# The second feed-forward of an attention and two feed-forward kernel moved into the list scheduler as single operations

## The chip, the cores and the metric

One core of a Trainium2 chip runs the whole program. The metric is the device time of one execution in microseconds; of several executions the median is given. Engine names follow the profile: PE is TensorE, DVE is VectorE, ACT is ScalarE, POOL is GpSimd, SP is SyncE, which issues nearly all DMAs here.

## The reference

Linear attention without a softmax, an RMS norm, a feed-forward with the maximum of three products, and a second feed-forward with a squared ReLU:

```python
kv = np.einsum('bhsd,bhse->bhde', k, v)            # batch 8, heads 8, seq 576, head_dim 64
out = np.einsum('bhsd,bhde->bhse', q, kv)
rms = np.sqrt(np.mean(out * out, axis=-1, keepdims=True) + 1e-06)
x = out / rms * g_norm                             # then 4608 tokens x 512
h = np.maximum(np.maximum(x @ w1, x @ w2), x @ w3) # 512 x 768
x = h @ w_out                                      # 768 x 512
h = x @ w_in                                       # second feed-forward, 512 x 2048
g = s * np.maximum(h, 0.0) ** 2 + b
return g @ w_out                                   # 2048 x 512
```

## The kernel before

All products are made in three matmuls of rounded parts: each operand is split into a high part (ScalarE copies it into the shorter format, `hi_part`, or the first half of `split`, L160) and a low part (the difference, `lo_part`, or the second half of `split`, L161), and a product is high x high + high x low + low x high.

**The first part** (attention and first feed-forward) works on nine blocks of 512 token columns, 22 positions each. Every operation is a *job* (L70): a position, an engine, a price in us, a function, and the names it reads, writes and allocates. `arrange` (L73) is a list scheduler: it derives the dependencies, keeps a clock for each engine, and takes at every step, on the engine that can begin first, the ready job with the lowest position. An allocation in a ring of n slots (`SIZE`) depends on the users of the one n before it. A job's end is its begin plus its price plus a lag (2.0 us for DMAs, 0.1 us otherwise, unless given). The order so found is issued with the order of PE, SP, DVE, ACT and POOL all kept as written (L138). Jobs with a position below `CUT` go there; this ends in the ninth block.

**The second feed-forward** uses a Strassen scheme with seven products instead of eight. *The w_in stage*: 20 groups `G`, four weight groups g for each of five pairs of token blocks (four pairs 512 columns wide, the last block's pair 256). `left` makes weight operands from a 1 MB load of `wd[g]` (`q_load`), `x_sums` and `right` make token operands from `x1_load`, `product` (L880) does one of seven products in 12 matmuls, `combine` (L897) empties its accumulators: products 0 to 2 are copied to `cs` by ScalarE, products 3 to 5 are added to these copies by VectorE, then ReLU and square, and `keep` stores the result in `gd`. There are two sets of four PSUM banks; within a group products 0, 2, 4 and 6 use the bank pair "a" one after another, so product 6 waits for the adds of product 4. `bias_load`, `bias_add`, `bias_sums` and `bias_out` add up rows of w_out in the middle of this stage. *The w_out stage*: ten halves `H` (eight 512 wide, two 256 wide), seven products of 24 matmuls. `z_load` brings the kept results back, `z_right` (L950) makes one operand in one of six slots `HS` (for products 2 and 3 with a sum on VectorE before), and every sixth low part is done by GpSimd (L960). `z_product` (L962) multiplies; `z_combine` (L975) adds up. In odd halves GpSimd also adds the earlier half's result to the copies of products 0 to 2 (L991). `put` (L1032) transposes a finished pair on VectorE and stores it in four DMAs; for the last, half-wide pair it turns it by matmuls on PE.

All of this was entered by `at(position, function)` in the hand-written list `plan`. `run` (L135) sorts it by position together with the jobs left over from the first part, and issues it with only the order of PE and SP kept (L142); the order of DVE, ACT and POOL is found by the language's own scheduler at compile time.

Of the kernel before, what the change touches and what calls it, by code (L numbers as in the profile page):

```python
# [30 lines left out]
def attention_max_ffn_relu2_ffn(ctx: ExitStack, tc, q, k, v, g_norm, w1, w2, w3, wo, wi, w2o, s, b, out):  # L31
# [14 lines left out]
    B, H, S, D = q.shape  # L46
    DM = H * D
# [16 lines left out]
    plan, jobs = [], []  # L64
    SIZE = {"g": 4, "t": 2, "st": 2, "qt": 2, "o": 2, "kvc": 3, "k": NP, "v": NP, "cgc": 2}

    def at(pos, fn, *args):
        plan.append((pos, len(plan), fn, args))
# [4 lines left out]
    def arrange(todo):  # L73
# [5 lines left out]
        for n, (_, _, _, _, _, _, r, w, a, _) in enumerate(todo):  # L79
# [18 lines left out]
            deps = {d for d in deps if d[0] != n}  # L98
# [4 lines left out]
        for n, e in enumerate(todo):  # L103
            if not need[n]:
                for eng in e[2].split("/"):
                    heaps.setdefault(eng, []).append(n)
# [25 lines left out]
        assert len(out) == len(todo)  # L132
        return [todo[n] for _, n in out]

    def run():  # L135
        order = sorted(jobs, key=lambda e: e[:2])
        n = sum(e[0] < CUT for e in order)
        with tc.manual_schedule(engines={EngineType.PE, EngineType.SP, EngineType.DVE, EngineType.Activation, EngineType.Pool}):  # L138
            for e in arrange(order[:n]):
                e[4](*e[5])  # L140
        todo = sorted(plan + [(e[0], e[1] - len(jobs), e[4], e[5]) for e in order[n:]], key=lambda e: e[:2])
        with tc.manual_schedule(engines={EngineType.PE, EngineType.SP}):  # L142
            for _, _, fn, args in todo:
                fn(*args)
# [415 lines left out]
    def plan_conv(kk, src, pos, load, a, pr, slot=None, store=None):  # L560
# [11 lines left out]
        if store is None:  # L572
            job(pos, "ACT", 0.63, conv_hi, key, slot, r=[tr + ":t"], w=[f"W_{kk}:0"], a=[(slot, f"W_{kk}")])
            job(pos, "DVE", 0.69, conv_lo, key, r=[tr + ":t", f"W_{kk}:0"], w=[f"W_{kk}:1"])
        else:
            job(store, "SP", 1.1, conv_store, key, r=[tr + ":t"])
# [114 lines left out]
    def plan_g2_out(j, n, pos):  # L691
        job(pos, "ACT", 0.6, g2_out, j, n, r=[f"g2.{j}.{n}"], w=[f"x1.{j}.{n}"], a=[("st", f"x1.{j}.{n}")])
        job(pos + 0.2, "SP", 1.1, x1_store, j, n, r=[f"x1.{j}.{n}"])
# [84 lines left out]
    XS = ["l0", "l1", "l6", "l7", "l2", "l3", "l4", "l5"] + HS  # L778

# [9 lines left out]
    def bank(parity, nm):  # L789
        return (psg, p2["psum"])[parity % 2].tile([P, N], F32, tag="g", name=nm)  # L790

    def tmp(nm):
        return p2["pool"].tile([P, N], F32, tag="c", bufs=6, name=nm)

    turn = [0]

    def stage2(nm):
        turn[0] += 1
        return base.tile([P, N], F32, tag=("t", "st")[turn[0] % 2], bufs=2, name=nm)
# [4 lines left out]
    add, sub = ALU.add, ALU.subtract  # L804
# [3 lines left out]


    def q_load(g, into):  # L810
        raw = into()
        st["wq", g] = raw
        if len(raw) == 1:
            nc.sync.dma_start(out=raw[0], in_=wd[g])
        else:
            for i, r in enumerate(raw):
                nc.sync.dma_start(out=r, in_=wd[g][:, 2 * i:2 * i + 2])

    def quarter(g, n):
        raw = st["wq", g]  # L820
        return raw[0][:, n] if len(raw) == 1 else raw[n // 2][:, n % 2]

    def left(g, i):
        a11, a12, a21, a22 = (quarter(g, n) for n in range(4))
        s_ = st.setdefault(("S", g), {})

        def make(n, x, op, y):
            s_[n] = tmp(f"s{n}_{g}")
            tt(nc.vector, s_[n], x, op, y)

        if i == 1:
            make(3, a11, sub, a21)
        elif i == 2:
            make(1, a21, add, a22)
            make(2, s_[1], sub, a11)
            make(4, a12, sub, s_[2])
        f = {0: a11, 3: a22, 5: a12}.get(i)
        f = s_[{1: 3, 2: 2, 4: 1, 6: 4}[i]] if f is None else f
        w = wt["q", g, i] = slot(WS[g % 4][i], f"w_q_{g}_{i}")
        split(w[:, 0], w[:, 1], f, nc.vector)  # L840
# [3 lines left out]
    def width(q):  # L844
        return N if q < NQ - 1 else N // 2

    def x1_load(q):
        n = width(q)
        raw = [base.tile([P, KD, N], F32, tag=tg, name=f"{tg}1_{q}") for tg in ("xh", "xl")]
        for i, r in enumerate(raw):  # L850
            src = x1d[2 * q + i] if q < NQ - 1 else x1d[2 * q][:, :, i * n:(i + 1) * n]
            nc.sync.dma_start(out=r[:, :, :n], in_=src)
        p2["raw", q] = raw

    def x_sums(q, k):
        n = width(q)
        b11, b12, b21, b22 = (p2["raw", q][c][:, r * HK + k, :n] for r in range(2) for c in range(2))
        t3, t2, t4 = (tmp(f"t{m}_{q}_{k}")[:, :n] for m in (3, 2, 4))
        tt(nc.vector, t3, b22, sub, b12)
        tt(nc.vector, t2, t3, add, b11)  # L860
        tt(nc.vector, t4, b21, sub, t2)
        tt(nc.vector, b12, b12, sub, b11)
        p2["t", q, k] = (b11, t3, t2, t4, b12, b21, b22)

    def right(q, i, k):

        n = width(q)
        if n == N:
            x = slot(XS[2 * i + k], f"x_q_{q}_{i}_{k}")
        else:  # L870
            if k == 0:
                p2["x2", i] = slot(XS[2 * i], f"x_q_{q}_{i}")
            x = p2["x2", i][:, :, k * n:(k + 1) * n]
        p2["x", q, i, k] = x
        f = p2["t", q, k][i]
        split(x[:, 0], x[:, 1], f, nc.vector)

    BANK = "abababca"[:5] + "ca"

    def product(G, q, g, i):  # L880
# [3 lines left out]
        for m in range(2):  # L884
            if new:
                st["ps", BANK[i], m] = bank(G + (i == 5), f"ps_{BANK[i]}_{G}_{m}")
        w = wt["q", g, i]
        for k in range(HK):
            x = p2["x", q, i, k]
            for m in range(2):  # L890
                ps = st["ps", BANK[i], m][:, :n]
# [5 lines left out]
    def combine(G, q, g, i):  # L897


        n = width(q)  # L900
        for m in range(2):
            ps = st["ps", BANK[i], m][:, :n]
            if i < 3:
                s_ = st["cs", i, m] = p2["pool"].tile([P, N], F32, tag="s", bufs=9, name=f"cs_{G}_{i}_{m}")[:, :n]
                act(out=s_, in_=ps, func=AF.Copy)  # L905
                continue
            if i < 6:
                h = st["cs", 5 - i, m]
                tt(nc.vector, h, ps, add, h)
            else:  # L910
                h = stage2(f"r_{G}_{m}")[:, :n]
            if i < 6 and m == 0:
                stt(out=h, in0=h, scalar=0.0, in1=h, op0=ALU.max, op1=ALU.mult)
            else:
                act(out=h, in_=ps if i == 6 else h, func=AF.Relu)
                act(out=h, in_=h, func=AF.Square)
            st["r", i, m] = h
            if i == 6:
                d = st["r", 7, m] = stage2(f"d_{G}_{m}")[:, :n]
                tt(nc.vector, d, st["r", 4, m], sub, h)  # L920
                tt(nc.vector, h, h, sub, st["r", 5, m])

    def keep(q, g, i):
        for m in range(2):
            nc.sync.dma_start(out=gd[q][:, {5: 0, 4: 1, 3: 2, 7: 3, 6: 4}[i], 2 * g + m, :width(q)], in_=st["r", i, m])
# [6 lines left out]
    def z_load(H, i, u):  # L932
# [4 lines left out]
        t = tmp(f"z_{H}_{u}") if i == 1 else slot(GS[i][u], f"z_{H}_{i}_{u}", F32)  # L937
# [12 lines left out]
    def z_right(H, i, k_):  # L950
        n, z = width(H // 2), lambda i_: p2["z", H, i_, k_]
        if i in (2, 3):
            if i == 2:
                tt(nc.vector, z(1), z(1), add, z(0))
            else:
                tt(nc.vector, z(1), z(5), sub, z(1))
        f = z(1 if 0 < i < 4 else i)
        o = 28 * H + 4 * i + k_
        x = hs["z", i, k_] = slot(HS[o % M1], f"zx_{o}")
        split(x[:, 0, :n], x[:, 1, :n], f, nc.gpsimd if o % 6 == 5 else nc.vector)  # L960

    def z_product(H, i, k_):  # L962
        n, new = width(H // 2), i in (0, 1, 5)
        kk = 4 * (H % 2) + k_
        w, x = wt["q", 4 + kk // 2, i], hs["z", i, k_]
        for m in range(2):
            if new and k_ == 0:
                st["ps", BANK[i], m] = bank(H + (i == 5), f"zs_{BANK[i]}_{H}_{m}")
            ps = st["ps", BANK[i], m][:, :n]
            c = slice((2 * (kk % 2) + m) * P, (2 * (kk % 2) + m + 1) * P)  # L970
            for e, (a, b_) in enumerate(((0, 0), (0, 1), (1, 0))):
                nc.tensor.matmul(ps, lhsT=w[:, a, c], rhs=x[:, b_, :n], start=new and k_ == 0 and e == 0,  # L972
                                 stop=k_ == 3 and e == 2, skip_group_check=True)

    def z_combine(H, i):  # L975
        n, more = width(H // 2), H % 2

        def acc(i_, m):
            c = int(i_ in (4, 6))
            if ("o", H // 2, c) not in p2:  # L980
                tg = ("xh", "xl")[c]
                p2["o", H // 2, c] = base.tile([P, KD, N], F32, tag=tg, name=f"{tg}o_{H}")
            return p2["o", H // 2, c][:, 2 * (i_ in (3, 4)) + m, :n]

        for m in range(2):
            ps = st["ps", BANK[i], m][:, :n]
            if i < 3:
                s_ = st["cs", i, m] = p2["pool"].tile([P, N], F32, tag="s", bufs=9, name=f"zc_{H}_{i}_{m}")[:, :n]
                act(out=s_, in_=ps, func=AF.Copy)  # L989
                if more:  # L990
                    tt(nc.gpsimd, s_, s_, add, acc(5 - i, m))  # L991
            elif i < 6:
                tt(nc.vector, acc(i, m), ps, add, st["cs", 5 - i, m])
            elif more:
                tt(nc.vector, acc(i, m), ps, add, acc(i, m))
            else:
                act(out=acc(i, m), in_=ps, func=AF.Copy)
            if i > 2 and more:
                act(out=acc(i, m), in_=acc(i, m), func=AF.Identity, scale=sb_s,  # L999
# [148 lines left out]
```

## Time and profile before

| | |
|---|---|
| median of three executions | 1399.04 us (1398.34 to 1402.06) |
| the profiled execution | 1398.18 us, span in the profile 1396.3 us |
| PE busy | 1370.8 us, 98% of the span |
| DVE busy | 890.1 us, 64% |
| ACT busy | 745.9 us, 53% |
| POOL busy | 235.7 us, 17% |
| granted PE clock | full in all of the span but its last slices |
| DMA | 202.51 MB, 145 GB/s on average |

The page gives each engine's busy time, the share in slices of the span, and groups of instructions with their mean duration and the idle time before them. A matmul's record overlaps with the next one's: the start-to-start distance is its pace, the record is longer. A line number can be that of a helper: L802 is every `tt` (add or subtract), L160 and L161 are the two halves of `split`.

### The profile page before, as it was taken

How to read it: one execution, taken by the hardware profiler on the slowest of the kernel's cores; microseconds unless marked ns; L12 is line 12 of the kernel's file. 1: busy time of each engine (PE TensorE's matmuls, PEld its weight loads, DVE VectorE, ACT ScalarE, POOL GpSimd, SP SyncE). 2: the span in 40 equal slices, each digit the busy share in tenths (PEclk: the TensorE clock that was granted, in tenths of full speed). 3: DMA queues.
4: the chain of work that ended last, by engine and by line, in shares of the span. 5: the costliest groups of instructions: out<-in, count | busy, mean ns of one | idle time of the engine just before them, and what ended most of it. 6: DMA issues, size and time to landing. Idle time of an engine off the chain costs nothing. (4 is left out here: it accounts for less than half of the span.)

```text
span 1396.3 us, 19558 instructions
## 1 busy us (share of the span) xinstructions
PE 1370.8 (98%) x7056; PEld 1121.7 (80%) x7056; DVE 890.1 (64%) x1413; ACT 745.9 (53%) x1320; POOL 235.7 (17%) x175
## 2 busy tenths in 40 slices
PE   7999999999999999999999899999999999999997
PEld 4777888888888888888888789887888888888887
DVE  5984636263635462454756757568877978888884
ACT  6864424342524353333646466556675656566565
POOL 0001213131212222211000000000012314141412
PEclk9999999999999999999999999999999999999999
DMA  9987281818364321030355635544684454544441
GB/s 281 269 178 146 83 171 46 190 55 174 71 163 83 98 68 38 1 121 17 142 196 188 226 135 199 181 151 163 214 296 152 143 194 152 193 140 145 158 143 38
DMA packets 221328, 202.51 MB, mean 145 GB/s; under 512 B 117168, under 2 KB 175536, under 8 KB 219056
## 3 DMA queue, kind: packets, MB, share of 16 engines
q1 hardware_dynamic: 221072, 201.02, 48.7%
q8 instruction: 55, 0.90, 0.3%
q14 instruction: 41, 0.34, 0.1%
q10 hardware_dynamic: 160, 0.26, 0.0%
HBM read 126.79 MB, written 74.45 MB: 144 GB/s over the span
## 5 line engine op out<-in xcount | busy, mean ns | idle before, releaser
L164 PE MATMUL g<-xh,w_w 128*128 128x512 f32 x648 | 255.2, 394 | 0.0
L166 PE MATMUL g<-xh,w_w 128*128 128x512 f32 x648 | 252.9, 390 | 0.7 <-DVE w_w L285 0.7
L165 PE MATMUL g<-xl,w_w 128*128 128x512 f32 x648 | 252.6, 390 | 0.0
L160 ACT ACTIVATE zx<-z 128x512 fp32r<-128x512 f32 (+1 forms) x280 | 161.2, 587 | 123.1 <-PE zs_a L972 34.2
L894 PE MATMUL ps_a<-x_q,w_q 128*128 128x512 f32 (+1 forms) x960 | 209.9, 370 | 4.2 <-DVE cs L802 4.1
L972 PE MATMUL zs_a<-zx,w_q 128*128 128x512 f32 (+1 forms) x960 | 203.9, 369 | 0.5 <-POOL zx L161 0.3
L894 PEld LDWEIGHTS ps_a<-x_q,w_q 128*128 128x128 f32 x960 | 167.4, 188 | 37.9 <-DVE cs L802 6.7
L161 DVE TENSOR_TENSOR zx<-z,zx 128x512 fp32r<-128x512 f32 (+1 forms) x234 | 172.2, 753 | 34.7 <-ACT zx L160 34.3
L972 PEld LDWEIGHTS zs_a<-zx,w_q 128*128 128x128 f32 x960 | 167.8, 188 | 32.1 <-POOL zx L161 0.7
L534 DVE TENSOR_TENSOR h<-g,h 128x512 f32<-128x512 f32 x108 | 74.6, 691 | 143.0 <-PE g L166 139.0
L161 POOL TENSOR_TENSOR zx<-z,zx 128x512 fp32r<-128x512 f32 (+1 forms) x46 | 64.2, 1397 | 592.4 <-DMA gd<-cs 380.9
L164 PEld LDWEIGHTS g<-xh,w_w 128*128 128x128 f32 x648 | 121.6, 188 | 27.4 <-issue 0.8
L166 PEld LDWEIGHTS g<-xh,w_w 128*128 128x128 f32 x648 | 121.6, 188 | 27.0 <-DVE w_w L285 1.2
L165 PEld LDWEIGHTS g<-xl,w_w 128*128 128x128 f32 x648 | 121.7, 188 | 25.2 <-DVE xl L285 0.2
L285 POOL TENSOR_TENSOR h<-h,h 128x512 fp32r<-128x512 f32 x40 | 55.1, 1378 | 454.8 <-ACT h L282 454.8
L894 PE MATMUL ps_b<-x_q,w_q 128*128 128x512 f32 (+1 forms) x480 | 106.4, 369 | 1.8 <-ACT cs L905 1.2
L282 ACT ACTIVATE h<-h 128x512 fp32r<-128x512 f32 x54 | 34.0, 630 | 134.5 <-DVE h L534 133.7
L972 PE MATMUL zs_b<-zx,w_q 128*128 128x512 f32 (+1 forms) x480 | 103.9, 371 | 2.0 <-DVE zx L161 2.0
L972 PEld LDWEIGHTS zs_b<-zx,w_q 128*128 128x128 f32 x480 | 83.9, 188 | 19.0 <-DVE zx L161 3.2
L894 PEld LDWEIGHTS ps_b<-x_q,w_q 128*128 128x128 f32 x480 | 83.9, 188 | 18.3 <-ACT cs L905 1.9
L164 PE MATMUL g<-h,w_o 128*128 128x512 f32 x216 | 84.6, 392 | 0.0
L165 PE MATMUL g<-h,w_o 128*128 128x512 f32 x216 | 84.1, 389 | 0.0
(176 smaller groups left out, 1980.3 us busy)
## 6 DMA issues: line engine op xcount, KB each, us to landing
z<-gd SPq DMA_DIRECT2D x64, 512.0 KB
gd<-cs SPq DMA_DIRECT2D x96, 256.0 KB
z<-gd SPq DMA_DIRECT2D x48, 256.0 KB
x1d<-x SPq DMA_DIRECT2D x36, 256.0 KB
raw_w<-in_moe_w_dram SPq DMA_DIRECT2D x18, 511.0 KB
k<-in_k_dram SPq DMA_DIRECT2D x32, 256.0 KB
v<-in_v_dram SPq DMA_DIRECT2D x32, 256.0 KB
wd<-tr_p SPq DMA_DIRECT2D x32, 256.0 KB
```

The source lines that it names most:

```text
L160: act(out=hi, in_=src, func=AF.Copy)
L161: eng.tensor_tensor(out=lo, in0=src, in1=hi.bitcast(F32), op=ALU.subtract)
L164: nc.tensor.matmul(ps, lhsT=w[:, 0, sl], rhs=xh, start=first, stop=False)
L165: nc.tensor.matmul(ps, lhsT=w[:, 0, sl], rhs=xl, start=False, stop=False)
L166: nc.tensor.matmul(ps, lhsT=w[:, 1, sl], rhs=xh, start=False, stop=last)
L282: act(out=out, in_=src, func=AF.Copy)
L285: eng.tensor_tensor(out=out, in0=src, in1=hi.bitcast(F32), op=ALU.subtract)
L534: nc.vector.tensor_tensor(out=st["h", m], in0=ps, in1=st["h", m], op=ALU.max)
L894: nc.tensor.matmul(ps, lhsT=w[:, a, c], rhs=x[:, b_], start=new and k == 0 and e == 0, stop=k == HK - 1 and e == 2, skip_group_check=True)
L972: nc.tensor.matmul(ps, lhsT=w[:, a, c], rhs=x[:, b_, :n], start=new and k_ == 0 and e == 0, stop=k_ == 3 and e == 2, skip_group_check=True)
```

## The change

`plan`, `at` and the second half of `run` go away. Every operation of the second feed-forward becomes a job of its own, with price, names read, written and allocated; the functions are cut into single operations for that (`split` into `left_hi` and `left_lo`, `combine` into `comb_copy`, `comb_add`, `comb_sq`, `comb_d` and `comb_e`, and so on). `arrange` gets a second argument: the jobs before it are done and only give names. Engine orders of all five engines are now kept in the second part too. Positions stay as they were, but for `z_right`, which goes from 2.4 to 3 ahead of its product. In `z_lo` and in the sums of `z_comb` VectorE takes GpSimd's place. In the half-wide halves two operands share one of the six slots `HS`.

```diff
-    def arrange(todo):
+    def arrange(todo, done=0):
...
-            deps = {d for d in deps if d[0] != n}
+            deps = {d for d in deps if done <= d[0] != n} if n >= done else ()
...
-            if not need[n]:
+            if n >= done and not need[n]:
...
-        todo = sorted(plan + [(e[0], e[1] - len(jobs), e[4], e[5]) for e in order[n:]], key=lambda e: e[:2])
-        with tc.manual_schedule(engines={EngineType.PE, EngineType.SP}):
-            for _, _, fn, args in todo:
-                fn(*args)
+            open_late()
+            for e in arrange(order, n):
+                e[4](*e[5])
...
+    def cost(eng, n):
+        return {"ACT": 0.62, "DVE": 0.69, "POOL": 1.35}[eng] if n == N else {"ACT": 0.43, "DVE": 0.42, "POOL": 0.75}[eng]
...
+    def plan_q_load(pos, g, *tags):
+        two = len(tags) > 1
+        job(pos, SQ_, 3.4, q_load, g, tags, r=[f"wd{g}:{n}" for n in range(4)], w=[qk(g, n) for n in range(4)],
+            a=[(tag, f"wq{g}{'ab'[i]}") for i, tag in enumerate(tags)], lag=3.0)
...
+        job(pos, A, 0.62, left_hi, g, i, r=[f], w=[w + ":0"], a=[(WS[g % 4][i], w)])
+        job(pos, V, 0.69, left_lo, g, i, r=[f, w + ":0"], w=[w + ":1"])
...
+            job(pos, SQ_, 3.4 if q < NQ - 1 else 1.7, x1_load, q, i, r=[f"x1d{j}:{n}" for n in range(KD)],
+                w=[f"xr{q}.{i}:{r}{k}" for r in range(2) for k in range(HK)], a=[(("xh", "xl")[i], f"xr{q}.{i}")], lag=3.0)
...
+        job(pos, "PE", 2.73 if width(q) == N else 1.44, product, G, q, g, i, r=[f"WQ{g}.{i}:0", f"WQ{g}.{i}:1", *xk], w=names,
+            a=[(parity(G + (i == 5)), nm) for nm in names] if new else [])
...
+    def comb_add(G, q, i, m):
+        h = st["cs", G, 5 - i, m]
+        tt(nc.vector, h, st["ps", G, BANK[i], m][:, :width(q)], add, h)
...
+            job(pos, SQ_, 0.85 if width(q) == N else 0.45, keep, G, q, g, i, m, r=[src], w=[f"gd{q}:{ORD[i]}.{2 * g + m}"])
...
             if i < 6:
-                h = st["cs", 5 - i, m]
-                tt(nc.vector, h, ps, add, h)
+                job(pos, V, cost(V, n), comb_add, G, q, i, m, r=[ps], w=[c])
...
-        split(x[:, 0, :n], x[:, 1, :n], f, nc.gpsimd if o % 6 == 5 else nc.vector)
+            job(pos, V, cost(V, n), z_sum, H, i, k_, r=[z(0 if i == 2 else 5)], w=[z(1)])
+        f, x = z(1 if 0 < i < 4 else i), z_x(H, i, k_)
+        new = n == N or k_ % 2 == 0
+        job(pos, A, cost(A, n), z_hi, H, i, k_, r=[f], w=[x + "h"],
+            a=[(HS[(o if n == N else o // 2) % M1], x.split(":")[0])] if new else [])
+        eng = V
+        job(pos, eng, cost(eng, n), z_lo, H, i, k_, eng, r=[f, x + "h"], w=[x + "l"])
...
+        job(pos, "PE", 1.365 if width(H // 2) == N else 0.72, z_product, H, i, k_,
...
-                if more:
-                    tt(nc.gpsimd, s_, s_, add, acc(5 - i, m))
+                job(pos, A, cost(A, n), z_comb, H, i, m, 0, r=[ps], w=[c], a=[("s", c)])
                 if more:
+                    job(pos, V, cost(V, n), z_comb, H, i, m, 1, r=[o(5 - i, m)], w=[c])
...
+            job(t + (0 if g == 4 else 2 * n - 1.9), SQ_, 3.4, bias_load, g, r=[f"wd{g}:{i}" for i in range(4)],
+                w=[f"B{g}:{i}" for i in range(4)], a=[(("xl", "xh")[g == 4], f"B{g}")], lag=3.0)
+            for i in range(4) if n else ():
+                job(t + 2 * n - 0.6, V, 0.69, bias_add, g, i, r=[f"B{g}:{i}"], w=[f"B4:{i}"])
...
+        if q < NQ - 1:
+            job(pos, V, 0.78, put, H, c, u, tag, r=o, w=[nm], a=[(tag, nm)])
+            job(pos + 0.05, SQ_, 1.4, put_store, H, c, u, r=[nm])
+            return
+        job(pos, "PE", 1.0, turn_mm, c, u, r=[*o, "unit"], w=["T" + nm], a=[(parity(u), "T" + nm)])
...
-                at(t + 2 * n + 0.5 * kk - 2.4, z_right, H, i, kk)
-                at(t + 2 * n + 0.5 * kk, z_product, H, i, kk)
-            at(t + 2 * n + 1.9, z_combine, H, i)
+                plan_z_right(t + 2 * n + 0.5 * kk - 3, H, i, kk)
+                plan_z_product(t + 2 * n + 0.5 * kk, H, i, kk)
+            plan_z_combine(t + 2 * n + 1.9, H, i)
```

## Rows read from the trace of the kernel before

**Rows 1.** The page, part 1: busy us (share of the span) x instructions.

```profile
PE 1370.8 (98%) x7056; PEld 1121.7 (80%) x7056; DVE 890.1 (64%) x1413; ACT 745.9 (53%) x1320; POOL 235.7 (17%) x175
```

**Rows 2.** Busy time by stretch: bounds, length, engines' busy us (instructions), clock, DMA.

```profile
100.00:650.00 550.00, 550.00 (x2898) 446.43 (x2897) 265.73 (x397) 216.57 (x359) 123.80 (x88) 1.00 0.40 97
650.00:1036.00 386.00, 380.02 (x1820) 317.10 (x1819) 260.32 (x452) 232.70 (x441) 1.52 (x2) 1.00 0.52 184
1036.00:1340.00 304.00, 303.30 (x1328) 248.88 (x1327) 249.84 (x334) 187.29 (x311) 96.99 (x64) 1.00 0.51 166
1340.00:1388.00 48.00, 44.90 (x355) 43.19 (x355) 34.52 (x80) 29.69 (x76) 11.79 (x14) 1.00 0.20 55
```

**Rows 3.** Waits of PE from 650 us on: total us, times, longest; the first row.

```profile
PE ps_a L894 <- DVE cs L802: 4.1, 5, 1.8
```

**Rows 4.** Timeline of PE: start us, us, engine, line, operation, tiles, count.

```profile
676.37 2.92 PE L894 MATMUL ps_a<-x_q,w_q 128*128 128x512 f32 x12
...
698.77 2.91 PE L894 MATMUL ps_b<-x_q,w_q 128*128 128x512 f32 x12
701.52 2.91 PE L894 MATMUL ps_a<-x_q,w_q 128*128 128x512 f32 x12
...
1032.95 5.71 PE L972 MATMUL zs_a<-zx,w_q 128*128 128x512 f32 x24
```

**Rows 5.** The chain that ended last: start us, us, what; w_out stage.

```profile
1099.90 5.44 PE zs_c L972 x24
...
1121.87 5.55 PE zs_a L972 x24
...
1346.83 2.87 PE zs_a L972 x24
...
1388.10 0.02 issue
```

**Rows 6.** Timeline of all engines around PE's longest wait of the w_in stage.

```profile
756.77 0.87 SPq L1006 DMA_DIRECT2D wb<-wd  x2
...
764.14 0.69 DVE L802 TENSOR_TENSOR cs<-ps_b,cs 128x512 f32<-128x512 f32 x1 [5.60 <-PE ps_b L894]
...
767.63 2.50 DVE L802 TENSOR_TENSOR wb<-wb,wb 128x512 f32<-128x512 f32 x4 [2.79 <-DMA wb<-wd]
...
771.25 1.28 DVE L802 TENSOR_TENSOR cs<-ps_a,cs 128x512 f32<-128x512 f32 x2
...
771.99 5.80 PE L894 MATMUL ps_a<-x_q,w_q 128*128 128x512 f32 x24 [1.80 <-DVE cs L802]
```

**Rows 7.** Waits of DVE for loads, 650 to 1036 us: total us, times, longest.

```profile
DVE s L802 <- DMA wq<-wd: 11.6, 5, 4.1
...
DVE t L802 <- DMA xl<-x1d: 8.8, 3, 5.4
DVE wb L802 <- DMA wb<-wd: 6.8, 2, 4.0
```

**Rows 8.** Timeline, w_out stage: POOL's adds and DVE's beside them.

```profile
1160.20 3.28 POOL L802 TENSOR_TENSOR zc<-zc,xlo 128x512 f32<-128x512 f32 x2
1160.55 3.48 DVE L802 TENSOR_TENSOR z<-z,z 128x512 f32<-128x512 f32 x2
```

**Rows 9.** Instruction groups, 1036 to 1340 us: count, busy us, mean ns, idle before.

```profile
L161 DVE TENSOR_TENSOR zx<-z,zx 128x512 fp32r<-128x512 f32 x182 | 146.4, 821 | 31.5 <-ACT zx L160 31.4
L802 DVE TENSOR_TENSOR z<-z,z 128x512 f32<-128x512 f32 x64 | 58.6, 934 | 2.9 <-POOL zx L161 2.4
...
L161 POOL TENSOR_TENSOR zx<-z,zx 128x512 fp32r<-128x512 f32 x37 | 56.8, 1536 | 561.5 <-DMA gd<-cs 380.9 <-ACT zx L160 172.9 <-DMA z<-gd 7.6
```

**Rows 10.** Waits of DVE, 1036 to 1340 us, the largest.

```profile
DVE zx L161 <- ACT zx L160: 31.8, 53, 2.0
```

**Rows 11.** The half-wide stretch: a DVE group from 1340 us, SP's timeline.

```profile
L1049 DVE STREAM_TRANSPOSE o<-xlo 128x512 f32<-128x512 f32 x4 | 2.8, 708 | 2.1 <-DMA out_dram<-o 2.1
...
1338.39 22.57 SPq L1057 DMA_DIRECT2D out_dram<-o  x32
```

## Predicted, before the changed kernel ran

> **What bounds the kernel now.** I began with the engines' busy time [rows 1]: TensorE (PE) is busy for 98% of the span, VectorE 64%, ScalarE 53%, GpSimd 17%. Then the busy time by stage [rows 2]: from 100 to 650 us, where every engine's order comes from the list scheduler, PE has no idle time at all (550.00 of 550.00); from 650 to 1036 (the products with w_in) it lacks 386.00 - 380.02 = 5.98 us, from 1036 to 1340 (w_out, full width) 0.70 us, from 1340 to 1388 (w_out, half width) 3.10 us. So PE sets the time, and whatever this change brings lies in those gaps.
>
> A matmul's record overlaps the next one's, so idle time read this way is too short. The pitch shows more. Twenty-four matmuls of 512 columns take 5.44 us where nothing holds them, and 24 of 256 columns 2.87 us [rows 5]. The w_in stage has 16 groups of seven products of 12 matmuls at full width and 4 groups at half width: 16 x 7 x 2.72 + 4 x 7 x 1.435 = 344.8 us. It lasts from 676.37 to 1032.95 [rows 4], 356.6 us: 11.8 us more. The w_out stage needs 8 x 7 x 5.44 + 2 x 7 x 2.87 = 344.8 us and lasts from 1032.95 to 1388.10 [rows 4, 5], 355.15 us: 10.3 us more. Not all of that is waiting. Some blocks run a little slower without an idle row: 5.55 instead of 5.44 us [rows 5], and in the first stage 701.52 - 698.77 = 2.75 instead of 2.72 us [rows 4]. With 16 such blocks in the second stage (1.7 us) and 60 in the first (1.8 us), and some 3 us of bias and transposing matmuls in both stages together (estimated at 0.12 us each from the 2.87 us for 24), about 9 us of the first excess and 6.5 us of the second are waits: **15.5 us is all there is to win**. After 1388.10 the end is a chain of VectorE, ScalarE, PE and store that the change leaves as it is.
>
> **Where the w_in waits come from.** In the timeline around the longest one [rows 6], two 1 MB loads of bias rows are issued at 756.77. VectorE adds one half of product 3 to its copy at 764.14; the next instruction in its queue is an add of the loaded rows, and it stands there until 767.63, four of them 2.50 us long. The adds that free the accumulator "a" sit behind it; the second pair starts at 771.25, and PE, which wants that bank for product 6, starts at 771.99 after 1.80 us idle. This is head-of-queue blocking, by order, not lack of VectorE time. VectorE waits like this for three loads: weights 11.6 us, bias rows 6.8 us, x1 8.8 us [rows 7], and PE's waits for its adds in cs sum to 4.1 us [rows 3], the largest entry.
>
> **The change, part by part.**
>
> *1. VectorE, ScalarE and GpSimd follow the list scheduler too.* The same instructions with the same matmuls, so PE's work is unchanged. An add of loaded rows is now placed where the list's clock says that the load has landed, and PE may take a later product that is ready first. The prices behind that clock agree with the rows: 2.73 us against 2.72 for a product, 0.69 for an add against 0.69 alone and 0.62 in a run of four [rows 6]. The first part shows what such a list does [rows 2]: no PE gap in 550 us. I take 7 of the 9 us. What could remain is a load later than its price. The list gives two 1 MB loads 2 x 3.4 + 3.0 = 9.8 us; the rows show 767.63 - 756.77 = 10.9 us [rows 6], 1.1 us late. PE has 2.72 us (product 5) between product 4 and the reuse of its bank, the two adds take 1.3 us, so 1.4 us is free, and a late load costs nothing or some 0.3 us. With about ten loads the bounds are 0 and 3 us; I take 1 us, nearer the row that fits into the slack.
>
> *2. SP's order.* Every DMA of this part (10 stores of 256 KB a group, the loads of weights, x1, z and bias, the output stores) moves in SP's queue to where the list puts it, so a store that waits for its data holds the loads behind it. z tiles are freed some 8 positions (about 22 us at 2.72 us each) before they are needed again, which covers this, at no cost. At half width a position lasts half as long, and there one price is clearly wrong: an output store of four DMAs costs 1.4 us in the list, but 32 of them take 22.57 us [rows 11], 2.8 us for four. By the eighth the real queue is 8 x 1.4 = 11.2 us behind the list, and VectorE's transposes, placed by the list, stand waiting for their two-slot rings; they waited 2.1 us before [rows 11]. Behind them are the low parts that feed PE. Part 4 covers up to 8.6 us of it: bounds 0 and 2.6 us, taken 1 us.
>
> *3. w_out's GpSimd work on VectorE.* 37 low parts in the full-width stretch [rows 9] and the 24 adds of sums there (6 in each of four odd halves) come over: 61 x 0.69 = 42.1 us more for VectorE in 304 us. It is paid back. When GpSimd runs two adds in 3.28 us, VectorE's two beside them take 3.48 us [rows 8] instead of 1.28 for two [rows 6]. Over the stretch VectorE's low parts average 821 ns and its sums 934 ns [rows 9], so without GpSimd it gets back 182 x 0.13 + 64 x 0.24 = 39 us. Busy time stays at 249.8 + 42.1 - 39 = 253 of 304 us [rows 2], 83%. The same holds at half width. Net cost taken: 0.
>
> [...]
>
> *4. Half-wide operands share a slot.* Two operands in one of six slots make up to 12 ready ones, 12 x 0.72 = 8.6 us of work ahead of PE instead of 4.3 us. The 6.5 us of waits in the w_out stage lie mostly at half width (3.10 us of idle rows against 0.70) [rows 2]. With this lead, with low parts that no longer wait for GpSimd's longer ones, and with PE not stopping in front of the transposing matmuls while a product is ready, I take 3 of 6.5 us.
>
> *5. The seam.* The second list starts with all engines free and all earlier work done. Engines really arrive at different times; the first product comes at 676.37 [rows 4], a whole row-block later, so this costs 0, with 1.5 us as the upper end (two adds behind one another).
>
> **Sum.** -7 - 3 + 1 + 1 = -8 us. The profiled execution took 1398.18 us (span 1396.3 and 1.9 us around it), so it becomes 1390.2; the median of the runs lies 0.86 us above that execution, which gives **1391.0 us**. Its own range: everything won, 1399.0 - 15.5 = 1383.5; only 4.5 won, 1394.5.
>
> **Rivals.**
>
> *The loads, not the order, are late (no change).* VectorE's 27.2 us of waiting for loads [rows 7] is then data that arrives late in any order, and the same adds block the same queue. For it: the two loads came 1.1 us later than the list assumes. Against: between 764.14 and 767.63 [rows 6] the loads' adds could have stood behind the adds that PE waits for; only their place in the queue put them first. Then w_in gains some 2 us, w_out 1.5, new waits cost 2: 1397.5 us.
>
> *VectorE becomes the bound of the w_out stage (slower).* In a fixed order each low part stands until its high part on ScalarE is done. VectorE waits 31.8 us for that in the full-width stretch now [rows 10]; with 253 us of work, 19 us are left. This rival decides from the point where those waits pass 51 us. If they double to 64, the stretch is 253 + 64 - 304 = 13 us longer, and half width, 48 us of the same kind, 2 us: 15 - 7 - 1 = 7 us slower, 1406 us. Where: blocks 2 and 3 of each half, in which every operand also needs a sum, so 16 adds x 0.69 = 11.0 us stand against 10.9 us of PE, while eight transposes fall in the same place. Against it: six slots are a lead of up to 8.2 us, and adds in a run take 0.62 us. [...]
>
> *The list repeats the hand order,* because both sort by the same positions: 1399 us. Against it: the list puts nothing in front of its modelled arrival.
>
> **How the numbers follow.** Forecast 0.65, loads late 0.20, VectorE as bound 0.12, same order 0.03. A difference of 0.3% (4.2 us) is about what a measurement of this kernel can tell from no change. Faster: 0.65. Within: 0.20 + 0.03 = 0.23. Slower: 0.12. The range starts at 1384.5, just above the floor of 1383.5, and reaches through "loads late" and a mild form of the bound on VectorE to 1400.
>
> **What the new profile would show.** Right: PE busy within 2 us of the stretch between 676 and about 1024; VectorE's waits for loads below 15 us, and none with cs adds behind it; no GpSimd work but the identity; z sums and low parts at 690 ns; VectorE 80 to 85% busy in w_out. Wrong: PE waiting for VectorE's zx by more than a microsecond in each half; transposes waiting for output stores by more than 5 us in all with PE idle behind them; PE gaps that follow late weight loads. What would upset the sum most is a list whose clock runs away from the real one, so that a queue head waits where no row of before shows a wait.

## Result and profile after

| | before | after |
|---|---|---|
| median of the executions | 1399.66 us (1398.34 to 1402.06, 4) | 1387.06 us (1386.75 to 1387.90, 4) |
| profiled execution | 1398.18 us, span 1396.3 | 1386.89 us, span 1385.1 |
| ratio to before | | 0.9909, 95% interval 0.9892 to 0.9926 |

The kernel became faster by 12.6 us. The forecast was 1391.0 us; the direction and the place were right, the size was too small.

Busy time of the changed kernel by the same stretches as [rows 2] (bounds, length, busy us of PE, PEld, DVE, ACT and POOL, clock, DMA share, GB/s):

```profile
650.00:1036.00 386.00, 386.00 (x1855) 324.15 (x1853) 269.76 (x463) 238.78 (x450) 1.29 (x1) 1.00 0.52 189
1036.00:1340.00 304.00, 304.00 (x1363) 251.46 (x1362) 250.39 (x401) 186.69 (x320) 0.61 (x2) 1.00 0.51 161
```

PE has no gap left from 650 to 1340 us, where it had 5.98 and 0.70 us. All that it still waits for in this part is at the beginning of the half-wide halves (total us, times, longest):

```profile
PE zs_b L1101 <- DVE zx L282: 2.0, 2, 1.3
PE zs_a L1101 <- DVE zx L282: 0.4, 1, 0.4
```

The first and last starts of the products give the two stages' lengths (line, duration min/median/max in ns, first and last start):

```profile
L947 PE MATMUL ps_a<-x_q,w_q x960: 274/389/480, 677.6 to 1025.8; 128*128 128x512 f32 x153, 128*128 128x256 f32 x39
L1101 PE MATMUL zs_a<-zx,w_q x960: 276/389/398, 1026.0 to 1376.9; 128*128 128x512 f32 x154, 128*128 128x256 f32 x38
```

From first start to first start the w_in stage takes 1026.0 - 677.6 = 348.4 us, where it took 356.6 [rows 4]: 8.2 us less. The w_out stage takes 1376.9 - 1026.0 = 350.9 instead of 355.2 us [rows 4, 5]: 4.3 us less. From there to the end of the span it is 8.2 us in both kernels. The first product starts 1.3 us later than before (677.64 against 676.37 us). This is no work of the change: PE's hundredth matmul already starts that much later (14.38 against 13.13 us), and over the runs below the first product scatters by as much (676.4 to 677.8 us in all but two).

A good half of the w_out stage's 4.3 us lies at the matmuls that transpose the half-wide result on PE (`turn`). Ahead is the kernel before, then the changed one:

```profile
1379.23 0.61 PE L1038 MATMUL turn<-unit,xho 128*128 128x128 f32 x4
1380.65 0.49 PE L1038 MATMUL turn<-unit,xho 128*128 128x128 f32 x2 [0.80 <-ACT xho L999]
...
1382.45 2.39 PE L972 MATMUL zs_a<-zx,w_q 128*128 128x256 f32 x18
```

```profile
1373.29 1.06 PE L1220 MATMUL turn<-unit,xho 128*128 128x128 f32 x8
1374.11 3.11 PE L1101 MATMUL zs_a<-zx,w_q 128*128 128x256 f32 x24
```

Before, sixteen of them and two waits keep PE from its products for 1382.45 - 1379.23 = 3.22 us. Now eight of them take 0.82 us there; the other eight come after the last product, where the end takes 8.2 us as before. That is 2.4 us less in the stage.

What took the place of the blocked queue of [rows 6] is seen in the timeline around the same loads:

```profile
756.83 0.38 SPq L1160 DMA_DIRECT2D wb<-wd  x1
...
764.93 1.37 DVE L803 TENSOR_TENSOR cs<-ps_b,cs 128x512 f32<-128x512 f32 x2 [2.73 <-issue]
...
767.60 1.37 DVE L803 TENSOR_TENSOR cs<-ps_a,cs 128x512 f32<-128x512 f32 x2 [0.70 <-PE ps_a L947]
768.08 2.88 PE L947 MATMUL ps_c<-x_q,w_q 128*128 128x512 f32 x12
769.49 2.49 DVE L803 TENSOR_TENSOR wb<-wb,wb 128x512 f32<-128x512 f32 x4
770.80 4.50 PE L947 MATMUL ps_a<-x_q,w_q 128*128 128x512 f32 x19
```

The adds that free the accumulators now stand before the adds of the loaded rows, in pairs, and the loaded rows are there when their turn comes. PE goes from product 5 to product 6 without a gap. From 650 to 1036 us VectorE waits for loads twice, 1.3 us in all, where it waited 27.2 us [rows 7]; the 0.8 us lie within the w_in stage:

```profile
DVE t L803 <- DMA xh<-x1d: 0.8, 1, 0.8
...
DVE t L803 <- DMA xl<-x1d: 0.5, 1, 0.5
```

In the w_out stage its operations have their undisturbed length, against 821 and 934 ns in [rows 9] (1029 to 1333 us, as long after the stage's beginning as there; count, busy us, mean ns, idle before):

```profile
L282 DVE TENSOR_TENSOR zx<-z,zx 128x512 fp32r<-128x512 f32 x218 | 146.8, 688 | 50.2 <-ACT zx L279 45.9 <-DMA z<-gd 0.7
L803 DVE TENSOR_TENSOR z<-z,z 128x512 f32<-128x512 f32 x64 | 42.6, 684 | 0.4
```

### The profile page after: what moved, and what is told of

Read it like the earlier page. It is cut to its first block, busy times and chain, and to the rows that moved or that the text cites. A ratio compares the mean times of both kernels' runs of the same rounds, so it can differ in the third digit from the quotient of the medians.

```text
span 1385.1 us, 19411 instructions
## 1 busy us (share of the span) xinstructions
PE 1367.6 (99%) x7056; PEld 1122.9 (81%) x7056; DVE 894.0 (65%) x1489; ACT 741.7 (54%) x1320; POOL 127.1 (9%) x99
## 4 chain that ended last, share of the span: by engine, by line
PE 96%; DVE 2%; ACT 1%; DMA 1%; issue 0%; SPq 0%; ACTq 0%; DVEq 0%
PE ps_a L947 14%; PE g L161 14%; PE zs_a L1101 14%; PE g L163 14%; PE g L162 14%; PE ps_b L947 7%; PE zs_b L1101 7%; PE ps_c L947 4%; PE zs_c L1101 4%; PE kvor L334 1%; PE ops L403 1%; PE ms L438 0%; PE ms L439 0%; PE qps L370 0%; DVE tr_w L255 0%; DMA out_dram<-o 0%
## 5 line engine op out<-in xcount | busy, mean ns | idle before, releaser
L279 ACT ACTIVATE zx<-z 128x512 fp32r<-128x512 f32 (+1 forms) x280 | 158.3, 586 | 123.9 <-PE zs_a L1101 37.6
L1101 PE MATMUL zs_a<-zx,w_q 128*128 128x512 f32 (+1 forms) x960 | 212.0, 369 | 0.4 <-DVE zx L282 0.4
L947 PEld LDWEIGHTS ps_a<-x_q,w_q 128*128 128x128 f32 x960 | 167.6, 188 | 31.8
L1101 PE MATMUL zs_b<-zx,w_q 128*128 128x512 f32 (+1 forms) x480 | 109.4, 370 | 2.0 <-DVE zx L282 2.0
L161 PE MATMUL g<-h,w_o 128*128 128x512 f32 x216 | 84.6, 392 | 0.0
L162 PE MATMUL g<-h,w_o 128*128 128x512 f32 x216 | 84.1, 389 | 0.0
L163 PE MATMUL g<-h,w_o 128*128 128x512 f32 x216 | 84.1, 389 | 0.0
```

The costliest lines, as they stand in the source:

```text
L161: nc.tensor.matmul(ps, lhsT=w[:, 0, sl], rhs=xh, start=first, stop=False)
L162: nc.tensor.matmul(ps, lhsT=w[:, 0, sl], rhs=xl, start=False, stop=False)
L163: nc.tensor.matmul(ps, lhsT=w[:, 1, sl], rhs=xh, start=False, stop=last)
L279: act(out=out, in_=src, func=AF.Copy)
L947: nc.tensor.matmul(ps, lhsT=w[:, a, c], rhs=x[:, b_], start=new and k == 0 and e == 0, stop=k == HK - 1 and e == 2, skip_group_check=True)
L1101: nc.tensor.matmul(ps, lhsT=w[:, a, c], rhs=x[:, b_], start=new and k_ == 0 and e == 0, stop=k_ == 3 and e == 2, skip_group_check=True)
```

## Experiments

Stage lengths are taken as above, from the profiled execution. Each ratio compares with runs of the kernel before on the same chip (their medians: 1398.8 to 1400.3 us). The intervals of two variants overlap where their medians lie 1 or 2 us apart; such a pair is read from the stage length and the waits too. The profiled execution need not be the median one.

| run | median us | ratio (interval) | w_in us | w_out us |
|---|---|---|---|---|
| before | 1399.66 | | 356.6 | 355.2 |
| after | 1387.06 | 0.9909 (0.9892 to 0.9926) | 348.4 | 350.9 |
| e2_before_no_pool | 1396.05 | 0.9969 (0.9957 to 0.9981) | 357.7 | 352.8 |
| e3_after_two | 1403.83 | 1.0023 (1.0010 to 1.0036) | 356.1 | 357.1 |
| e4_after_pool | 1385.91 | 0.9902 (0.9887 to 0.9916) | 348.4 | 350.3 |
| e5_no_sharing | 1388.43 | 0.9918 (0.9901 to 0.9935) | 348.3 | 352.3 |
| e6_loads_cheap | 1409.43 | 1.0066 (1.0044 to 1.0088) | 367.5 | 351.0 |
| e7_store_28 | 1387.23 | 0.9917 (0.9903 to 0.9932) | 348.4 | 351.0 |
| e8_pe_in_order | 1387.87 | 0.9920 (0.9905 to 0.9935) | 349.4 | 350.9 |
| e9_pool_store_28 | 1385.58 | 0.9903 (0.9888 to 0.9917) | 348.4 | 350.0 |
| e10_more_slots | 1387.90 | 0.9920 (0.9907 to 0.9934) | 348.4 | 351.4 |
| e11_pool_unpriced | 1388.26 | 0.9928 (0.9915 to 0.9942) | 348.4 | 352.2 |
| e12_pool_slots | 1388.62 | 0.9928 (0.9915 to 0.9940) | 348.3 | 353.0 |
| e13_less_transposes | 1384.28 | 0.9891 (0.9868 to 0.9915) | 348.4 | 348.2 |

### Whose order makes the gain: VectorE's or PE's

**e3_after_two.** The list's order for PE and SP alone:

```diff
+        with tc.manual_schedule(engines={EngineType.PE, EngineType.SP}):
             open_late()
             for e in arrange(order, n):
                 e[4](*e[5])
```

> The changed kernel, but in the second part only PE and SP keep the list's order; the order of VectorE, ScalarE and GpSimd is again found by the language's scheduler. Theory (the gain in w_in comes from the order of VectorE's queue): the waits come back, VectorE waits for loads over 15 us (0.8 after the change), 1393 to 1396 us. Rival C (the new order of PE and SP, with products taken out of turn, does it): within 2 us of the changed kernel, 1387 to 1389.

It takes 1403.83 us, more than the theory's 1393 to 1396, and more than before. PE's waits in both stages, and VectorE's for loads in the first, are back:

```profile
PE zs_a L1102 <- DVE zx L283: 4.7, 5, 2.0
PE ps_a L948 <- DVE cs L804: 4.5, 4, 3.6
...
DVE s L804 <- DMA wq<-wd: 7.0, 3, 4.8
DVE t L804 <- DMA xl<-x1d: 6.2, 3, 3.5
DVE wb L804 <- DMA wb<-wd: 3.6, 3, 1.6
...
DVE t L804 <- DMA xh<-x1d: 1.6, 1, 1.6
```

Rival C is out: the list's order of PE and SP gives nothing by itself. VectorE waits for loads for 18.4 us in all. The edit frees ScalarE's and GpSimd's order as well as VectorE's, so it does not part these three; but of PE's 5.05 us of idle time in the w_in stage 4.5 us are waits for VectorE's adds.

That the whole is slower than before was not expected. The profiled execution (1400.42 us) is the second fastest of ten, so the stage lengths show only part of it. In the w_out stage, 1.9 us longer than before, the granted clock takes nearly as much: PE waits 2.05 us for a low part, and around the end of this wait the clock goes to the lower of its two levels, half (1.2 GHz), for 3.4 us (columns as above, 0.50 is the clock):

```profile
1350.18 4.45 PE L1102 MATMUL zs_a<-zx,w_q 128*128 128x256 f32 x23 [2.05 <-DVE zx L283]
```

```profile
1350.05:1353.46 3.41, 3.27 (x15) 3.28 (x16) 3.41 (x11) 0.89 (x3) 0.00 (x0) 0.50 0.29 87
```

About half of PE's 3.27 us there is lost, some 1.6 us (an estimate). Over the ten executions the mean granted clock is 0.995 to 0.999, in the four of the changed kernel 1.000. Another possible cause, that PE's order is found against a VectorE order that the kernel then does not use, is not tested.

**e8_pe_in_order.** PE kept to the positions inside the list:

```diff
+        last = []
...
+            if n >= done > 0 and todo[n][2] == "PE" and todo[n][4] is not turn_mm:
+                if last:
+                    deps.add((last[-1], True))
+                last.append(n)
```

> The changed kernel with PE held in the list to the order of the positions (the transposing matmuls at the end left free); the other engines' orders are found by the list as before. Theory (VectorE's order, not PE's freedom, makes the gain): the w_in stage at most 1.5 us longer, 1387 to 1389 us. Rival C (products taken out of turn make the gain): 4 us or more longer, 1391 and up.

1387.87 us, the w_in stage 1.0 us longer. Products taken out of turn are worth about 1 of the 8 us; the order of the other engines makes the rest. Two waits show where the freedom helps: without it VectorE stands for bias rows again and PE for an add.

```profile
PE ps_a L952 <- DVE cs L808: 1.0, 2, 0.6
...
DVE wb L808 <- DMA wb<-wd: 6.0, 2, 3.9
```

**e6_loads_cheap.** The list told that a load takes nearly nothing (the same edit for `x1_load` and `bias_load`; `x_sum` made to name only the tiles it needs):

```diff
-        job(pos, SQ_, 3.4, q_load, g, tags, r=[f"wd{g}:{n}" for n in range(4)], w=[qk(g, n) for n in range(4)],
-            a=[(tag, f"wq{g}{'ab'[i]}") for i, tag in enumerate(tags)], lag=3.0)
+        job(pos, SQ_, 0.3, q_load, g, tags, r=[f"wd{g}:{n}" for n in range(4)], w=[qk(g, n) for n in range(4)],
+            a=[(tag, f"wq{g}{'ab'[i]}") for i, tag in enumerate(tags)], lag=0.1)
```

> The changed kernel with the 1 MB loads of weights, bias rows and x1 priced in the list at 0.3 us with a lag of 0.1 us (3.4 or 1.7 and 3.0 before), so that VectorE's operations on them are placed where nothing has landed. Theory (what the list gains in w_in is that it knows when loads land): VectorE's waits for loads rise from 0.8 us to over 10 us, PE waits 2 to 6 us in the w_in stage, 1389 to 1393 us. Rival (PE takes other products meanwhile, or the old waits came from elsewhere): within 1 us of the changed kernel.

The theory's direction at nearly four times its size: 1409.43 us, 22 us above the changed kernel where 2 to 6 us were expected; the w_in stage 19 us longer, the w_out stage as after.

```profile
PE ps_a L948 <- DVE cs L803: 12.2, 5, 6.2
...
DVE s L803 <- DMA wq<-wd: 15.9, 4, 7.3
DVE t L803 <- DMA xl<-x1d: 12.4, 2, 6.9
DVE wb L803 <- DMA wb<-wd: 12.0, 3, 7.0
DVE t L803 <- DMA xh<-x1d: 9.4, 2, 4.8
```

VectorE waits 49.7 us for loads in this stage, and the add that PE needs is behind them; PE waits 12.2 us. Part of the rest is the granted clock again. Around the waits of 6.20 and 2.69 us it falls to the lower level, 6.8 us each time:

```profile
786.23 5.06 PE L948 MATMUL ps_a<-x_q,w_q 128*128 128x512 f32 x12 [6.20 <-DVE cs L803]
```

```profile
783.82:790.64 6.82, 4.42 (x10) 3.47 (x11) 5.34 (x9) 3.44 (x7) 0.00 (x0) 0.50 0.53 196
862.32:869.15 6.83, 6.16 (x29) 6.16 (x30) 6.83 (x16) 5.26 (x15) 0.00 (x0) 0.50 0.25 84
```

PE is busy for 10.6 us of these stretches and loses about half of that, some 5 us (an estimate); in the profiled executions of the kernel before and of the changed one the clock is full until the last slices. So it is the list's knowledge of when loads land that the w_in gain rests on, more than on listing as such: a list with wrong load times is 10 us worse than the order before, the slow clock included.

### GpSimd's work, and the shared slots

**e2_before_no_pool.** That part alone, on the kernel before:

```diff
-        split(x[:, 0, :n], x[:, 1, :n], f, nc.gpsimd if o % 6 == 5 else nc.vector)
+        split(x[:, 0, :n], x[:, 1, :n], f, nc.vector)
...
-                    tt(nc.gpsimd, s_, s_, add, acc(5 - i, m))
+                    tt(nc.vector, s_, s_, add, acc(5 - i, m))
```

> The kernel before, with nothing changed but GpSimd's 46 low parts and 30 adds of sums of the second feed-forward given to VectorE. Theory (the move is paid back by VectorE's shorter operations, the w_in waits have another cause): within 1.5 us of before, low parts and sums at 690 ns, w_in stage still 356 us long. Rival A (GpSimd's removal is what made w_out faster): the w_out stage about 4 us shorter, 1395 us. Rival B (VectorE becomes the bound of w_out): 4 us or more slower than before.

4.2 us faster: rival A, nearly. The w_out stage is 2.4 us shorter in the profile, whose execution (1397.23 us) was the second slowest of the six; where the rest of the 4.2 us lies is not shown. I had not expected a gain; the w_in stage did not gain, as the theory said (357.7 us; that it is 1.1 us longer goes with a granted clock of 0.50 from 800.73 to 804.14 us, after PE had waited 2.03 us for ScalarE).

**e4_after_pool.** The reverse, in the list:

```diff
-        eng = V
+        eng = G_ if o % 6 == 5 else V
...
-            tt(nc.vector, s_, s_, add, acc(H, 5 - i, m))
+            tt(nc.gpsimd, s_, s_, add, acc(H, 5 - i, m))
...
-                    job(pos, V, cost(V, n), z_comb, H, i, m, 1, r=[o(5 - i, m)], w=[c])
+                    job(pos, G_, cost(G_, n), z_comb, H, i, m, 1, r=[o(5 - i, m)], w=[c])
```

> The changed kernel with GpSimd's low parts (every sixth) and adds of sums back on GpSimd, as jobs of the list at 1.35 us (0.75 at half width). Theory (a neutral move in itself): 0 to 2 us slower than the changed kernel, 1387 to 1389. Rival A: 3 to 5 us slower, 1390 to 1392, with PE waiting for GpSimd's or VectorE's zx.

It is not slower but, by the medians, about 1 us faster than the changed kernel, 1385.91 us (1385.29 to 1387.41; the two overlap). PE's waits at half width fall from 2.4 to 1.2 us:

```profile
PE zs_b L1101 <- DVE zx L282: 0.8, 1, 0.8
PE zs_a L1101 <- DVE zx L282: 0.2, 1, 0.2
PE zs_a L1101 <- ACT zx L279: 0.2, 1, 0.2
```

**e11_pool_unpriced.** Why does GpSimd cost time in the old order and none in the list? The list adds 0.9 us to a VectorE operation that begins while GpSimd works. Here this is left out of the second part of e4:

```diff
-            if eng == "DVE" and begin < pool:
+            if eng == "DVE" and begin < pool and not done:
```

> GpSimd's low parts and adds of sums back on GpSimd, and the list's surcharge of 0.9 us for a VectorE operation that begins while GpSimd works left out in the second part. Theory (GpSimd does no harm in the list because the list knows how it holds VectorE up): the w_out stage 1 to 3 us longer than with the surcharge (350.3 us), 1387 to 1389 us. Rival G (six slots of lead absorb it either way): within 0.7 us of 1385.9.

The w_out stage grows from 350.3 to 352.2 us, PE's waits from 1.2 to 3.2 us, the median to 1388.26 us (the profiled execution, 1390.47 us, is the slowest of four). So the order that reckons with the hold-up is what made GpSimd harmless.

**e5_no_sharing.** One slot for each half-wide operand:

```diff
-        if n == N or k_ % 2 == 0:
-            st["zx", H, i, k_ // 2] = slot(HS[(o if n == N else o // 2) % M1], f"zx_{o}")
-        c = slice(0, N) if n == N else slice(k_ % 2 * n, (k_ % 2 + 1) * n)
-        x = hs["z", H, i, k_] = st["zx", H, i, k_ // 2][:, :, c]
+        x = hs["z", H, i, k_] = slot(HS[o % M1], f"zx_{o}")[:, :, :n]
...
```

> The changed kernel, but each half-wide operand of w_out takes a slot of its own again (6 operands ahead of PE, 4.3 us, instead of 12). Theory (the longer lead covers the transposes that wait for their stores): 2 to 4 us slower, 1389 to 1391, all of it after 1330 us, PE idle there 4 to 6 us instead of 2.4. Rival D (sharing plays no part, the list's order alone does): within 1 us of the changed kernel.

The w_out stage is 1.4 us longer, 1388.43 us: less than the theory's 2 to 4 and more than rival D's 1, and PE's idle rows are no longer than with sharing (2.4 us). Sharing is worth some 1.4 of the stage's 4.3 us.

### What is left at half width

**e7_store_28.** The price that the prediction called wrong, mended:

```diff
-            job(pos + 0.05, SQ_, 1.4, put_store, H, c, u, r=[nm])
+            job(pos + 0.05, SQ_, 2.8, put_store, H, c, u, r=[nm])
```

> The changed kernel with one output store of four DMAs priced at 2.8 us in the list instead of 1.4 us, the time that SP takes for it. Theory (the transposes at the head of VectorE's queue wait for their stores because the list thinks them done): these waits fall from 2.0 us to under 0.5, PE's idle time at half width from 2.4 to under 1 us, 1385 to 1386.5 us. Rival (VectorE is simply short of time at half width, the transposes only show it): within 0.5 us of the changed kernel's 1387.

1387.23 us: nothing. VectorE waits 2.1 us for stores (2.0 after), PE 2.5 us. In the halves ahead the stores and z loads change places in SP's queue; at half width VectorE's operations come in the same order as before the edit, and the 32 stores still go out in one run. So the price is not what makes the transposes wait; what their wait costs this run does not tell. The same price on top of e4, **e9_pool_store_28**:

> The two edits together: GpSimd's low parts and adds of sums back on GpSimd, and an output store priced at 2.8 us. Theory (both relieve the same place, VectorE's queue at half width, where PE still waits 1.2 us with GpSimd back): they hardly add up, 1385 to 1386 us. Rival (they act on different waits): 1384.5 us or less.

1385.58 us, 0.3 us from e4: within its expectation, and too little to tell from e4. It is the fastest complete version. The executions of e4 and e9 lie between 1384.40 and 1387.41 us, those of their two counterparts without GpSimd (the changed kernel and e7) between 1386.66 and 1388.67, which supports the 1 us of e4.

**e10_more_slots.** The last four transposes of the last full-width pair go to the ring of the copies, so that none of them waits for a store:

```diff
-        tag = either()
+        tag = "s" if q == NQ - 2 and c else either()
```

> The changed kernel, with the last four transposes of the last full-width pair written to the nine-slot ring of copies instead of the two rings of two, so that none of them has to wait for an output store. Theory E (the store that a transpose waits for is what stops VectorE and then PE at half width): VectorE's waits for output stores there go from 2.0 us to nearly none, PE's idle time from 2.4 to under 1 us, 1385 to 1386 us. Rival F (VectorE is short of time at that place, the waits only show it): PE still idle 1.5 us or more, 1386.5 to 1387.5.

VectorE's waits for stores are gone, but the w_out stage stays (351.4 us), at 1387.90 us, 0.4 us above rival F's range. PE is idle for 1.9 us instead of 2.4, and 0.7 us of that is a new wait, for a copy in the ring that the transposes now borrow. So theory E (under 1 us) is not borne out, though this run is no clean test of it. The row from 1333 to 1353 us, where half width begins, shows what took the place of the waits: VectorE is busy for 19.35 of 20 us. Ahead is the changed kernel's row, with the one for the next 20 us, then e10's:

```profile
1333.00:1353.00 20.00, 17.58 (x137) 16.72 (x136) 17.83 (x48) 12.59 (x37) 0.00 (x0) 1.00 0.29 85
1353.00:1373.00 20.00, 20.00 (x169) 20.00 (x168) 16.15 (x47) 11.24 (x33) 0.00 (x0) 1.00 0.08 24
```

```profile
1333.00:1353.00 20.00, 18.11 (x136) 16.58 (x135) 19.35 (x52) 12.65 (x36) 0.00 (x0) 1.00 0.29 87
```

**e12_pool_slots.** The edits of e4 and e10 together:

> GpSimd's work back on GpSimd, and the four transposes in the ring of copies. Theory E: PE's idle time at half width under 0.5 us, 1385 to 1385.6 us. Rival F: as with GpSimd's work back alone, 1385.9 us, since VectorE already has the time.

1388.62 us, slower than either expectation, w_out stage 353.0 us. The ring that the transposes borrow is that of the copies, and PE now waits 0.7 us for one (it did in e10 too). Whether this explains all of the 2.7 us over e4 stays open.

**e13_less_transposes.** Less work for VectorE at that place. A quarter of the last full-width pair's output is not made or stored, so its time is not that of a full kernel:

```diff
+        if q == NQ - 2 and c:
+            return
```

> The changed kernel without the last four transposes of the last full-width pair and without their output stores (a quarter of that pair's output is not written); everything else as it is. Rival F (VectorE is short of time where half width begins): 4 x 0.70 = 2.8 us less for VectorE there, PE's idle time at half width falls from 2.4 to under 0.8 us, 1384.5 to 1385.7 us. If neither VectorE's time nor the stores matter (the wait comes from the chain of high part, low part and slot): PE still idle over 1.5 us, within 0.7 us of 1387.

With 2.8 us less for VectorE, PE has no idle time from 1333 to 1353 us, the stage takes 348.2 us and the program 1384.28 us:

```profile
1333.00:1353.00 20.00, 20.00 (x164) 19.77 (x163) 18.30 (x51) 13.09 (x39) 0.00 (x0) 1.00 0.19 54
```

This run takes away stores as well as transposes; e10, which takes away only the waiting for stores, gained nothing. Together they point to VectorE's time. A rival stays untested: that the transposes only stand too early. PE needs the low parts behind them at once and the transposes not, and VectorE is busy for 16.15 of the next 20 us, so the 2.8 us would fit there; no run moves them.

## Why the prediction was right, and where it was off

**The bound.** Right: PE set the time, the waits in its way were the gain, and nothing fell below the floor of 1383.5 us.

**Part 1, w_in: 7 less 1 us forecast, 8.2 us measured.** The mechanism held point by point: the adds behind a load went in front of it, VectorE's waits for loads went from 27.2 to 1.3 us, and e6 brought the blocking back by wrong load times alone. The mis-sized term is the share: I took 7 of 9 us and 1 us for late loads. The stage now lasts 348.4 us without an idle row, its matmuls need 344.8, and the remaining 3.6 us are slow blocks and bias matmuls. So some 8.2 us, not 9, were waits, and all of them were won. The 1 us for late loads was not needed: VectorE hardly waits for one any more, and where it would have, PE can take another product (e8: 1 us).

**Part 2, SP's order: +1 us forecast, another cause measured.** VectorE's transposes did wait, 2.0 us, and PE behind them, as described. But the step "one price is clearly wrong, so the transposes wait, so PE waits" failed: with the right price the transposes stand where they did and wait as long (e7), and without the waits the time is no shorter (e10). At that place VectorE is short of time in the order it has: with four transposes and their stores less PE does not wait (e13). That the same work in another order would do is not tested. I had computed VectorE's share for the full-width halves (83%) and written that "the same holds at half width"; it does not, since the last full-width pair's eight transposes fall into halves that last half as long.

**Part 3, GpSimd's work: 0 forecast; +1 us here, -4 us in the old order.** The bookkeeping was right (39 us returned, 42 us added; VectorE busy 250 us where 253 were forecast). What it missed is that equal busy time is not equal time for PE. In an order that knows nothing of the hold-up, PE's products lose time to it (e2: 4.2 us by the medians, 2.4 us of it seen in the w_out stage); that it is VectorE's operations of 1.7 us each beside GpSimd [rows 8] that come late there is argued from these rows. In a list that prices the hold-up, GpSimd is spare capacity where VectorE is short (e4, e11). The Trainium skill, "Perfetto Trace Analysis", section "Optimizing Scalar/DVE Operations", says that work may go to GpSimd where VectorE is saturated; for half width e4 agrees with it, by 1 us.

**Part 4 and the w_out stage: 3 us forecast, 4.3 measured.** The third reason given, that PE no longer stops in front of the transposing matmuls, was the largest: 2.4 us, by the rows above (e2, without GpSimd but in the old order, still spends 2.07 us there). The other 1.9 us lie in the products, and GpSimd's move in the old order (e2) shortens the stage by as much as 2.4 us, so the shares overlap. Sharing keeps 1.4 us (e5): without it the gain would be 2.9.

**Part 5, the seam: 0,** as taken: no PE gap there.

**The sum.** -8.2 - 4.3 = -12.5 us by stages, -12.6 us by medians, where -8 was forecast. That the two agree is in part luck: the profiled executions differ by 11.3 us, since the changed kernel's first product came 1.3 us later. Against the forecast the two terms for new waits, +2 us, were too many, and the two gains 2.5 us too small.

**The rivals.** "The loads are late in any order" falls with the 1.3 us. "VectorE becomes the bound" was said to decide from 51 us of waiting for high parts in the full-width stretch. These waits did grow, from 31.8 [rows 10] almost to that point (the first line, for 1026 to 1333 us; 48.2 us in the stretch of [rows 10]):

```profile
DVE zx L282 <- ACT zx L279: 48.4, 83, 1.8
```

```profile
ACT zx L279 <- PE zs_a L1101: 34.7, 49, 1.3
```

and PE lost nothing there. The threshold was wrong in kind: VectorE runs ahead, and the high parts that it waits for wait in turn for PE to release a slot (the second line is the largest of three such, 58.6 us in all from 1036 to 1340 us), so this waiting is slack, not work. It is at half width, for 20 us and not for 304, that the rival came true, as far as VectorE's time is the cause there, for some 2.4 us.

## What to carry to other kernels

When the bounding engine is 98% busy, look behind its few waits for an instruction at the head of another engine's queue that waits for a load, and move it behind what the bounding engine needs. A list scheduler does that as well as its load times are: in the w_in stage it gained 8 us here with them and lost 11 without, some 5 of these at the lower clock that came with the longer waits. Before taking work off a slow helper engine, see whether its harm is its work or an order that does not reckon with it, and check the load of the engine that inherits the work in the shortest stage, not on average.

## What was not expected of the hardware

Two adds on GpSimd and two on VectorE side by side took 3.28 and 3.48 us [rows 8], against 1.28 for two alone, yet with the order fitted to it a kernel with 93 us of GpSimd work beside VectorE in the w_out stage (e4, 92.77 us from 1036 to 1340) was no slower than one with none. Waits of PE can cost more than their length: in e2, e3 and e6 the granted clock went to 0.50 for 3.4 or 6.8 us around waits of 2.03, 2.05, 2.2, 2.69 and 6.20 us.

The first part scatters more than the variants differ: the first w_in product starts between 676.4 and 677.8 us in all runs but two. In e11 it starts at 679.9 us: PE waits 2.3 us there for the first loads of v, and from 15.6 to 19.1 us the granted clock is 0.50. In e6, whose list also changes the ninth block, it starts at 682.1 us, after a wait of 2.2 us and 3.4 us at a clock of 0.50 (671.2 to 674.6).
